# PSUM banks of different tiles used side by side in the experts and the last layers

## The chip, the cores and the metric

The kernel runs on one core of a Trainium2 chip. The metric is the time of one execution on the device, in microseconds (us); the lower the better. The engines are named as the profile names them: PE is TensorE (PEld its weight load), DVE is VectorE, ACT is ScalarE, POOL is GpSimd, and SP issues the transfers.

## What is computed

Attention with rotary embedding over 4 batches, 8 heads, 576 tokens and 64 elements per head; a soft mixture of 8 experts with 4 slots each over the 2304 tokens; and a two-layer MLP of 512 to 2048 to 512 with a squared ReLU. All in float32.

```python
def _moe_ref(x, phi, w1, w2):
    logits = x @ phi                                   # 2304 x 32
    d = softmax over tokens of logits                  # (written out with max, exp, sum)
    slot_input = (d.T @ x).reshape(8, 4, 512)
    for e in range(8):
        h = np.maximum(slot_input[e] @ w1[e], 0.0)     # 4 x 1024
        slot_out[e] = h @ w2[e]                        # 4 x 512
    c = softmax over slots of logits
    return c @ slot_out                                # 2304 x 512

def _moe2_ref(x, w_in, w_out):
    r = np.maximum(x @ w_in, 0.0)
    return (r * r) @ w_out
```

(The two softmax lines are shortened.)

## The kernel before

**Stages.** Sixteen pairs of heads go through attention until about 331 us. The experts follow until about 392 us, and the MLP runs to the end at 624.5. A planner orders the program: every step is handed to `op` with its engines and estimated times, a due time and what it reads and writes, and the planner emits one order for each engine. The key `("b", i)` stands for PSUM bank i in these lists, so a step is ordered after whatever used its bank before. Below the planner, the programming layer adds the semaphore waits between engines.

**PSUM.** There are eight banks of 512 float32 values in each of the 128 partitions. `PAIRS` are three tiles of two banks each; `BANKS[0]` and `[1]` are the halves of the first, `[2]` and `[3]` of the second, `[4]` and `[5]` of the third. `BANKS[6]` and `[7]` are tiles of one bank. The printed orders name the tiles `bank0_86`, `bank1_87`, `bank2_88` (the three pairs) and `obank0_89`, `obank1_90`; the profile writes `bank` and `obank` and leaves the numbers out.

**Experts, first layer.** r runs over four pairs of experts. Each has four groups `m1` of eight matmuls (L1089, k = 0 to 3) into bank r % 2, then a ReLU eviction by ACT (L1106), four transposes `tr` by PE (L1114) into bank 2 + r % 2 and two copies `keep` by DVE (L1125) into `si`.

**Combination weights.** Between these, `combine(b)` makes the softmax over the slots of batch b, in bank 5 or 6: transposes of the logits (L889, L890), a chain of small DVE operations from L895 to L908 with an exponential on ACT (L923), transposes back (L913) and an ACT copy (L919).

**Experts, second layer.** `second(r)` has for each r four groups `m2` of eight matmuls (L1149) into bank r % 2, which a memset (L1133) has zeroed, an ACT copy (L1164) and a product `ms` with the group sum (L1170) into bank 4. A DVE copy (L1185) ends the stage. Idle fill matmuls (L1435) into a spare bank stand at places that the planner chose.

**MLP.** `w_prime` multiplies slot outputs by w_in (L1231, then ACT L1246, PE L1247, ACT L1248, DVE L1243) in bank 5. `mlp1` makes 768 tokens of one block of 128 hidden columns in two halves (L1295) and evicts them (L1306) before L1314, L1323, L1325 and L1340 square and split them. `mlp2` adds into six banks, c = 0 to 5, 36 matmuls a step (L1364), and after every fourth step the six banks are evicted: by ACT in the first of four quarters (L1380), by DVE with an addition after (L1386). The output leaves from L1392.

**Transfers.** SP issues the weights in one queue, in the planner's order. The last ones are w2 of the last pair into tEb and tEa, 512 KB each in two parts, and behind them six loads of w_in and w_out, 1024 KB each.

Of the kernel before, what the change touches and what calls it, by code (L numbers as in the profile page):

```python
# [14 lines left out]
AF = mybir.ActivationFunctionType  # L15
# [161 lines left out]
def kernel(  # L177
# [85 lines left out]
    def f(ap):  # L263
        return ap.bitcast(F32)
# [613 lines left out]
    def combine(b, g, mem):  # L878
        (lc_of, lc_k), (rm_of, _), (rs_of, _), (ck_of, ck_k) = mem
        lg = lgs[b]  # L880
        bank, bk = BANKS[5 + b % 2], [("b", 5 + b % 2)]
        lc = lc_of().rearrange("p (a s) -> p a s", s=NSLOT)
        rm, rs = rm_of().unsqueeze(2), rs_of().unsqueeze(2)
        ck = ck_of().rearrange("p (c g s) -> p c g s", c=5, g=4)

        lt = bank.rearrange("p (c s) -> p c s", s=NSLOT)

        def o0(e):
            nc.tensor.transpose(bank[:, 0:128], lg[:, 0:128], ident)  # L889
            nc.tensor.transpose(bank[0:64, 128:160], lg[0:NSLOT, 128:192], ident[0:NSLOT, 0:NSLOT])  # L890

        def o1(e):
            for a, cs in ((128, slice(0, 4)), (64, slice(4, 5))):
                t = lt[0:a, cs]
                nc.vector.tensor_reduce(out=rm[0:a, cs], in_=t, op=ALU.max, axis=AX.X)  # L895
                nc.vector.tensor_tensor(
                    out=lc[0:a, cs], in0=t, in1=rm[0:a, cs].to_broadcast(list(t.shape)), op=ALU.subtract
                )

        def o2(e):  # L900
            nc.vector.tensor_reduce(out=rs, in_=lc, op=ALU.add, axis=AX.X)
# [14 lines left out]

        def o4(t0, m):
            t0 += S * b
            nc.scalar.activation(out=cst_of()[:, t0 : t0 + m], in_=bank[:, 0:m], func=AF.Copy)  # L919

        op({"PE": 0.2}, o0, g, [("lg", b, n) for n in (4, 1)] + ["ident"], bk)
        op({"DVE": 0.8}, o1, g, bk, [lc_k])
        op({"ACT": 0.25}, lambda e: nc.scalar.activation(out=lc, in_=lc, func=AF.Exp), g, (), [lc_k])  # L923
        op({"DVE": 1.6}, o2, g, (), [lc_k, ck_k])
        for cs, t0, m in ((range(4), 0, 512), ((4,), 512, 64)):
            op({"PE": 0.11 * len(cs)}, lambda e, cs=cs: o3(cs), g, [ck_k, "ident"], bk)
            op({"ACT": 0.05 + m / 1100}, lambda e, t0=t0, m=m: o4(t0, m), g, bk, [("cst", b, t0)])
# [60 lines left out]
    def experts():  # L988
# [90 lines left out]

        for r in range(4):  # L1080
            w, wk, wslots = w_of("w1", r)
            bk = r % 2

            for k in range(4):

# [26 lines left out]
            def tr(e, hs_of=hs_of, bk=bk):  # L1112
                for k in range(4):
                    nc.tensor.transpose(  # L1114
                        BANKS[2 + bk][:, 128 * k : 128 * k + 128], hs_of()[:, 128 * k : 128 * k + 128], ident
                    )

            op({"PE": 0.5}, tr, g + r + 0.5, [hs_k, "ident"], [("b", 2 + bk)])

            def keep(e, bk=bk, r=r):  # L1120
                t = BANKS[2 + bk].rearrange("p (k j s) -> p k j s", k=4, j=4)
# [7 lines left out]
            op({"DVE": 0.25}, keep, g + r, [("b", 2 + bk), ht_k], [(ht_k, r)])  # L1129
        free("A1", g + 3.5, after=last)  # L1130

        for bk in range(2):
            op({"DVE": 0.5}, lambda e, bk=bk: nc.vector.memset(BANKS[bk], 0.0), g + 5, (), [("b", bk)])  # L1133
        for b in range(B):
            combine(b, g + 0.3 + 0.4 * b, cks[b % 2])

        def second(r):


            bk = r % 2  # L1140
            hs_of, hs_k = hs[bk]
            for j in range(4):
                w_of, wk, wslot = where["w2", 2 * r + j // 2, j % 2]

                def m2(e, j=j, w_of=w_of):
                    if r == 2:
                        spare_bank[:] = [aux[:, 0:128]]
                    for q in range(4):
                        nc.tensor.matmul(  # L1149
                            BANKS[bk][32 * q : 32 * q + 8, :],  # L1150
                            lhsT=ht_of()[:, r, q, 8 * j : 8 * j + 8],
                            rhs=w_of()[:, q, :],
                            start=(j == 0),
                            stop=(j == 3),
                        )
# [12 lines left out]
            def ms(e):  # L1168
                for k in range(4):
                    nc.tensor.matmul(  # L1170
                        BANKS[4][:, 32 * k + 8 * r : 32 * k + 8 * r + 8],
                        lhsT=hs_of()[:, 128 * k : 128 * k + 128],
                        rhs=gsum[:, 0:8],
                        start=True,
                        stop=True,
                    )

            op({"PE": 0.75}, ms, g + 10 + r, [hs_k], [("b", 4)], wait=WAIT)

        for r in range(4):  # L1180
            second(r)
        g += 30
        start = op(
            {"DVE": 0.2},
            lambda e: nc.vector.tensor_copy(out=sot, in_=BANKS[4][:, 0:128].rearrange("p (k s) -> p k s", k=4)),  # L1185
            g - 20, [("b", 4)], [("sit", 0), ("sit", 1)], wait=WAIT,
        )
        mlp(g + 2, sot, start)

# [4 lines left out]
    def mlp(g, sot, start):  # L1194
# [24 lines left out]
        def w_prime(n, due, c0=0, c1=512):  # L1219
# [20 lines left out]
            wk = sorted({wst_k(n, c // 128) for c in range(c0, c1, 128)}, key=str)  # L1240

            def low(e):
                nc.vector.tensor_tensor(out=o()[64:], in0=BANKS[5][64:, c0:c1], in1=f(o())[64:], op=ALU.subtract)  # L1243

            op({"PE": 0.1 + 0.85 * z}, m1, due, [("sit", 0), ("sit", 1)] + [cs[n % 2][h][1] for h in halves], [("b", 5)], wait=wait)
            op({"ACT": 0.05 + 0.45 * z}, lambda e: nc.scalar.activation(out=ws_of()[:, c0:c1], in_=BANKS[5][:, c0:c1], func=AF.Copy), due, [("b", 5)], [ws_k], wait=wait)  # L1246
            op({"PE": 0.02 + 0.85 * z}, lambda e: nc.tensor.matmul(BANKS[5][:, c0:c1], lhsT=gsum, rhs=ws_of()[:, c0:c1], start=True, stop=True), due, [ws_k], [("b", 5)], wait=wait)  # L1247
            op({"ACT": 0.05 + 0.45 * z}, lambda e: nc.scalar.activation(out=o(), in_=BANKS[5][:, c0:c1], func=AF.Copy), due, [("b", 5)], wk, wait=wait)  # L1248
            op({"DVE": 0.07 + 0.535 * z}, low, due, [("b", 5)], wk, wait=wait)

        def wst_k(n, q):
            return wst_key if n == 0 and q == 0 else ("wst", n, q // 2)
# [28 lines left out]
        def mlp1(n):  # L1281
# [6 lines left out]
            due, wait = (g + n - AHEAD, 0.0) if n else (g - 20, WAIT)  # L1288
            reads = [wst_k(fc // 4, fc % 4)] + [("cst", b, x) for b in range(B) for x in (0, 512)]
            for h in range(2):  # L1290
                i = 4 if one and n else 3 if one and h else 4 + h
                t0 = TT * t + 384 * h
                op(
                    {"PE": 0.17},
# [48 lines left out]
                    due, sk, gk, wait=wait,  # L1343
                )

        PO = [0, 1, 2, 3, 6, 7]

        def mlp2(n):
            q, t, fc = steps[n]
# [6 lines left out]
            for c in range(6):  # L1356

                def mm(e, c=c):
# [3 lines left out]
                    for i, (x, y) in enumerate(((0, 0), (0, 1), (1, 0))):  # L1362
                        for z in (slice(0, 256), slice(256, 512)):
                            nc.tensor.matmul(  # L1364
                                BANKS[PO[c]][:, z],
                                lhsT=gt[:, x, 128 * c : 128 * c + 128],
                                rhs=wo[:, fc % 2, y, z],
                                start=(fc % FQ == 0 and i == 0 and z.start == 0),
# [1 line left out]
                                skip_group_check=z.start > 0,  # L1370
                            )

                op({"PE": 0.7}, mm, g + n, [(gt_k, c // 3)] + wo_reads, [("b", PO[c])])
                if fc % FQ < FQ - 1:
                    continue
                o_of, o_k = sums[6 * t + c]
                if q == 0:
                    op(
                        {"ACT": 0.5},
                        lambda e, o_of=o_of, c=c: nc.scalar.activation(out=o_of(), in_=BANKS[PO[c]], func=AF.Copy),  # L1380
                        g + n, [("b", PO[c])], [o_k],
                    )
# [141 lines left out]
```

## Time and profile before

| | before |
|---|---|
| median of 3 runs | 629.14 us (625.99 to 629.26) |
| profiled execution | 626.27 us |
| its span in the trace | 624.5 us |
| PE busy | 94% |
| DVE, ACT, POOL busy | 62%, 45%, 35% |
| experts stage | about 338 to 392 us |
| MLP | about 392 to 624.5 us |

The span counts from the first to the last instruction of the trace; 1.8 us of the execution lie around it. The rows further down come from several views. A timeline row has a start, a duration, the engine, the line, the operation and its tiles, and a count of merged instructions; in brackets stands how long the engine was idle before and whom it waited for. The wait view adds up such idle times by line. The chain of work follows the work that ended last back through whatever released it. A window row has busy times of each engine in a stretch, then PE's clock, the DMA share and the rate.

### The profile page before, as it was taken

The numbers are of one execution on the slowest core, as the hardware profiler recorded it, in microseconds if no ns is written. First come the engines' busy times: TensorE is split into PE (matmuls) and PEld (weight loads), VectorE is DVE, ScalarE is ACT, GpSimd is POOL, SyncE is SP. The second block draws the span as 40 slices with busy tenths as digits, with TensorE's granted clock in tenths as the row PEclk, the third lists the DMA queues.
The fourth block names the chain that finished last, engine by engine and source line by source line (L and its number), as shares of the span: only waits on it lengthen the run. The fifth ranks groups of instructions, "written<-read, shape, count | busy, mean of one in ns | idle before, by whom it ended". The sixth has DMA issues, their size and how long they took to land.

```text
span 624.5 us, 13406 instructions
## 1 busy us (share of the span) xinstructions
PE 585.9 (94%) x5535; PEld 429.5 (69%) x5535; DVE 384.9 (62%) x818; ACT 278.9 (45%) x492; POOL 215.6 (35%) x168
## 2 busy tenths in 40 slices
PE   1899999999999999999997989999999999999997
PEld 1556555566555665555654324789999999999996
DVE  3476666766657666666534714998487569355543
ACT  1235444444344443453431313788484456444440
POOL 1999998538866668660110000000000000000000
PEclk9799999999999999999999999999999999999999
DMA  9546854574356331322538999333210030000222
GB/s 188 132 95 179 216 133 140 142 209 104 116 137 165 78 90 47 83 89 75 212 137 297 365 390 394 117 131 135 69 68 1 1 119 17 1 1 2 102 103 101
DMA packets 36253, 80.90 MB, mean 130 GB/s; under 512 B 7616, under 2 KB 8032, under 8 KB 35168
## 3 DMA queue, kind: packets, MB, share of 16 engines
q1 hardware_dynamic: 34704, 77.98, 40.9%
q10 hardware_dynamic: 1488, 2.06, 1.7%
q8 instruction: 43, 0.70, 0.5%
q14 instruction: 18, 0.15, 0.1%
HBM read 75.24 MB, written 4.72 MB: 128 GB/s over the span
## 4 chain that ended last, share of the span: by engine, by line
PE 73%; DMA 8%; DVE 7%; POOL 6%; ACT 2%; issue 2%; SPq 1%; ACTq 0%; DVEq 0%; POOLq 0%
PE bank L1364 21%; PE obank L1364 10%; PE obank L477 10%; PE bank L443 8%; POOL arena L320 4%; PE bank L495 4%; DMA arena<-in_qk_dram 3%; PE bank L391 3%; PE bank L1295 3%; PE bank L1149 2%; PE bank L447 2%; DVE mcol L398 2%; DMA tEb<-mrow 2%; PE bank L1089 2%; POOL tLb L320 1%
## 5 line engine op out<-in xcount | busy, mean ns | idle before, releaser
L456 ACT ACTIVATE tO<-bank 128x576 f32<-128x576 f32 (+1 forms) x160 | 99.5, 647 | 157.1 <-PE bank L447 136.4
L398 DVE TENSOR_REDUCE mcol<-bank 128x2 f32<-128x576 f32 x160 | 115.5, 748 | 53.3 <-PE bank L391 53.0
L320 POOL TENSOR_TENSOR arena<-arena 128x576 f32<-128x576 f32 x90 | 125.3, 1413 | 53.9 <-DMA arena<-in_qk_dram 53.6
L477 PE MATMUL obank<-tO,pb 128*64 128x288 f32 x640 | 104.8, 426 | 2.8 <-DVE pb L519 1.6
L1364 PE MATMUL bank<-w,tEb 128*128 128x256 f32 x576 | 72.8, 279 | 1.2 <-ACT w__927 L1380 1.1
L1364 PEld LDWEIGHTS bank<-w,tEb 128*128 128x128 f32 x576 | 70.0, 188 | 3.5 <-ACT w__927 L1380 1.4
L464 POOL TENSOR_TENSOR pb<-tO 128x576 f32<-128x576 f32 x32 | 45.2, 1413 | 36.8 <-ACT tO L456 36.8
L477 PEld LDWEIGHTS obank<-tO,pb 128*64 128x64 f32 x640 | 34.9, 135 | 31.8 <-issue 17.1
L1306 ACT ACTIVATE pb<-bank 128x384 f32<-128x384 f32 x48 | 22.1, 493 | 47.4 <-PE bank L1295 35.5
L501 DVE STREAM_TRANSPOSE bank<-bank 128x288 f32<-128x288 f32 x32 | 15.9, 498 | 44.2 <-PE bank L495 44.2
L495 PE MATMUL bank<-tO,ones 128*32 128x288 f32 x384 | 37.5, 410 | 0.0
L1364 PE MATMUL obank<-w,tEb 128*128 128x256 f32 x288 | 37.1, 277 | 0.0
L1306 ACT ACTIVATE arena<-bank 128x384 f32<-128x384 f32 x48 | 21.6, 489 | 33.1 <-PE bank L1295 31.4
L1364 PE MATMUL bank<-w,tEa 128*128 128x256 f32 x288 | 36.4, 280 | 0.0
L443 PE MATMUL bank<-tEb 64*128 64x288 f32 x200 | 35.5, 352 | 0.4 <-ACT tO L456 0.3
L1364 PEld LDWEIGHTS bank<-w,tEa 128*128 128x128 f32 x288 | 34.9, 188 | 1.4 <-issue 1.2
L1364 PEld LDWEIGHTS obank<-w,tEb 128*128 128x128 f32 x288 | 35.1, 188 | 0.0
L1364 PE MATMUL bank<-w,tO 128*128 128x256 f32 x288 | 35.0, 276 | 0.0
L1364 PEld LDWEIGHTS bank<-w,tO 128*128 128x128 f32 x288 | 34.6, 188 | 0.0
L443 PEld LDWEIGHTS bank<-tEb 64*128 64x128 f32 x200 | 18.7, 184 | 20.7 <-issue 11.3
L391 PE MATMUL bank<-tEb 64*128 64x288 f32 x200 | 29.7, 334 | 0.7 <-DVE mcol L398 0.5
L443 PE MATMUL bank<-tLb,tEb 64*128 64x288 f32 x200 | 29.5, 292 | 0.0
(286 smaller groups left out, 1097.2 us busy)
## 6 DMA issues: line engine op xcount, KB each, us to landing
arena<-in_qk_dram SPq DMA_DIRECT2D x15, 576.0 KB
arena<-in_qk_dram SPq DMA_DIRECT2D x14, 512.0 KB
pb<-in_v_dram SPq DMA_DIRECT2D x16, 320.0 KB
arena<-in_w_dram SPq DMA_DIRECT2D x8, 512.0 KB
tLb<-in_w_in_dram SPq DMA_DIRECT2D x3, 1024.0 KB
pb<-in_w_in_dram SPq DMA_DIRECT2D x3, 1024.0 KB
w__415<-in_w_dram SPq DMA_DIRECT2D x4, 512.0 KB
w__591<-in_w_dram SPq DMA_DIRECT2D x4, 512.0 KB
```

What stands on the lines that cost most here:

```text
L320: ENG[e].tensor_tensor(out=o, in0=x, in1=y, op=how)
L391: nc.tensor.matmul(on_ring(tok)[:, j, 0:HQ], lhsT=hi[rows, 1, UNIT[u]], rhs=hi[rows, 0, HALF[h]], start=True, stop=True)
L398: lambda e: nc.vector.tensor_reduce(out=mcol[:, h, :, u], in_=on_ring(tok)[:, :, 0:HQ], op=ALU.max, axis=AX.X),
L443: nc.tensor.matmul(st[:, j, 0:HQ], lhsT=k[x][rows, UNIT[u]], rhs=q[y][rows, HALF[h]], start=(i == 0), stop=False)
L456: lambda e: nc.scalar.activation(out=pr[0:m], in_=on_ring(tok)[0:m, :, 0:HQ], func=AF.Exp, scale=0.125),
L464: lambda e: nc.gpsimd.tensor_tensor(out=acc, in0=one, in1=pr, op=ALU.add),
L477: nc.tensor.matmul(o_t[rows, 0:HQ], lhsT=vr[:, u, j, :], rhs=pr[:, j, :], start=(u == 0), stop=(u == 4))
L495: nc.tensor.matmul(sm[QUAD[2 * j + w], 0:HQ], lhsT=ones[:, 0:32], rhs=xs_[2 * i + w][:, j, :], start=(i == 0), stop=(i == 1))
L501: {"DVE": 0.47}, lambda e: nc.vector.transpose(out=on_ring(tok)[:, 1, 0:HQ], in_=on_ring(tok)[:, 0, 0:HQ]),
L1295: lambda e, i=i, t0=t0: nc.tensor.matmul(BANKS[i][:, 0:384], lhsT=wst_of()[:, 128 * fc : 128 * fc + 128], rhs=cst_of()[:, t0 : t0 + 384], ...
L1306: lambda e, i=i, h=h: nc.scalar.activation(out=rg_of()[:, 0, h], in_=BANKS[i][:, 0:384], func=AF.Relu),
L1364: nc.tensor.matmul(BANKS[PO[c]][:, z], lhsT=gt[:, x, 128 * c : 128 * c + 128], rhs=wo[:, fc % 2, y, z], start=(fc % FQ == 0 and i == 0 and ...
```

## The change

Only PSUM banks change, and the place of one memset. The first layer uses banks 0 and 2 in turn, and the transposes banks 1 and 3. `combine` takes the two one-bank tiles, 6 and 7, and its first step is also ordered after the second half of the slot inputs. The second layer takes banks 4 and 0 in turn; bank 4's memset is due ahead of combine, bank 0's stays with the later ones. `ms` and `w_prime` go to bank 7, `mlp1` to bank 6 in the first quarter (its very first step takes 5 as well) and to 6 and 7 after it, and `mlp2` to banks 0 to 5 in place of 0, 1, 2, 3, 6, 7.

```diff
@@ combine
-        bank, bk = BANKS[5 + b % 2], [("b", 5 + b % 2)]
+        bank, bk = BANKS[6 + b % 2], [("b", 6 + b % 2)]
...
-        op({"PE": 0.2}, o0, g, [("lg", b, n) for n in (4, 1)] + ["ident"], bk)
+        op({"PE": 0.2}, o0, g, [("lg", b, n) for n in (4, 1)] + ["ident", ("sit", 1)], bk)
@@ experts, first layer
-            bk = r % 2
+            bk = 2 * (r % 2)
...
-                        BANKS[2 + bk][:, 128 * k : 128 * k + 128], hs_of()[:, 128 * k : 128 * k + 128], ident
+                        BANKS[1 + bk][:, 128 * k : 128 * k + 128], hs_of()[:, 128 * k : 128 * k + 128], ident
...
-        for bk in range(2):
-            op({"DVE": 0.5}, lambda e, bk=bk: nc.vector.memset(BANKS[bk], 0.0), g + 5, (), [("b", bk)])
+        LATER = (4, 0)
+        for bk, due in zip(LATER, (g + 0.2, g + 2.2)):
+            op({"DVE": 0.5}, lambda e, bk=bk: nc.vector.memset(BANKS[bk], 0.0), due, (), [("b", bk)])
@@ second
-            bk = r % 2
-            hs_of, hs_k = hs[bk]
+            bk = LATER[r % 2]
+            hs_of, hs_k = hs[r % 2]
...
-                        spare_bank[:] = [aux[:, 0:128]]
+                        spare_bank[:] = [BANKS[2][:, 0:128]]
@@ ms, and the copy that ends the stage
-                        BANKS[4][:, 32 * k + 8 * r : 32 * k + 8 * r + 8],
+                        BANKS[7][:, 32 * k + 8 * r : 32 * k + 8 * r + 8],
@@ w_prime (all its uses of bank 5)
-                            BANKS[5][32 * k : 32 * k + 32, a:b],
+                            BANKS[7][32 * k : 32 * k + 32, a:b],
@@ mlp1
-                i = 4 if one and n else 3 if one and h else 4 + h
+                i = 6 if one and n else 5 if one and h else 6 + h
@@ mlp2 (PO[c] becomes c at all its uses)
-        PO = [0, 1, 2, 3, 6, 7]
-                                BANKS[PO[c]][:, z],
+                                BANKS[c][:, z],
```

The order of steps on each engine stays as it was but for one memset on DVE. What differs is the tiles and with them the waits. From line 1133 on, lines of the new kernel count one higher until the line `PO` is gone.

First place: PE at the first layer's r=1 (L1089 with w4 and w6 are k=0 and k=1, L1114 the transposes of r=0). Before:

```order
L1089 MATMUL bank0_86<-w4__1113,sit0_118 32x512 x2
L1089 MATMUL bank0_86<-w6__1473,sit0_118 32x512 x2
L1089 MATMUL bank0_86<-w4__1113,sit0_118 32x512 [waits Activation_49]
L1089 MATMUL bank0_86<-w4__1113,sit0_118 32x512
L1089 MATMUL bank0_86<-w6__1473,sit0_118 32x512 x2
L1114 MATMUL bank1_87<-ident_61,arena_76 128x128 [waits DMAHW7_49,DMAHW0_49]
L1114 MATMUL bank1_87<-ident_61,arena_76 128x128 x3
```

Now:

```order
L1089 MATMUL bank1_87<-w4__1113,sit0_118 32x512 x2
L1089 MATMUL bank1_87<-w6__1473,sit0_118 32x512 x2
L1089 MATMUL bank1_87<-w4__1113,sit0_118 32x512 x2
L1089 MATMUL bank1_87<-w6__1473,sit0_118 32x512 x2
L1114 MATMUL bank0_86<-ident_61,arena_76 128x128 [waits DMAHW7_49,DMAHW0_49,Activation_49]
L1114 MATMUL bank0_86<-ident_61,arena_76 128x128 x3
```

The wait for ACT has moved from the middle of r=1's first groups to the transposes behind them.

Second place: PE in the second layer, where the last group of r=0 is followed by the first of r=1 and by `ms` of r=0. Before:

```order
L1149 MATMUL bank0_86<-pb_84,si_66 8x512 [waits DMAHW1_49]
L1149 MATMUL bank0_86<-pb_84,si_66 8x512
L1149 MATMUL bank0_86<-pb_84,si_66 8x512 [waits DMAHW6_49,Activation_49]
L1149 MATMUL bank0_86<-pb_84,si_66 8x512
L1149 MATMUL bank0_86<-pb_84,si_66 8x512 [waits DMAHW7_49]
L1149 MATMUL bank0_86<-pb_84,si_66 8x512
L1170 MATMUL bank2_88<-gsum_62,arena_76 128x8 x4
```

Now (L1150 and L1171 are L1149 and L1170 of before):

```order
L1150 MATMUL bank2_88<-pb_84,si_66 8x512 [waits DMAHW1_49]
L1150 MATMUL bank2_88<-pb_84,si_66 8x512
L1150 MATMUL bank0_86<-pb_84,si_66 8x512 [waits DMAHW6_49,DVE_49]
L1150 MATMUL bank0_86<-pb_84,si_66 8x512
L1150 MATMUL bank0_86<-pb_84,si_66 8x512 [waits DMAHW7_49]
L1150 MATMUL bank0_86<-pb_84,si_66 8x512
L1171 MATMUL obank1_90<-gsum_62,arena_76 128x8 [waits Activation_49]
L1171 MATMUL obank1_90<-gsum_62,arena_76 128x8 x3
```

The wait for ACT stands at `ms` and no longer at r=1's first group, which now waits for DVE (the memset of bank 0).

Third place: DVE behind combine's last chain (L908 of b=3), with the copies L1125 of r=2 and r=3. Before:

```order
L908 TENSOR_TENSOR tEb2_120<-tEb2_120 128x5x32 [waits DVE_49]
L908 TENSOR_TENSOR tEb2_120<-tEb2_120 128x5x32
L1133 MEMSET bank0_86 128x512 [waits Activation_49]
L1125 COPY si_66<-bank1_87 128x4x2x4 [waits PE_49]
L1125 COPY si_66<-bank1_87 128x4x2x4
L1133 MEMSET bank0_86 128x512 [waits Activation_49]
L1125 COPY si_66<-bank1_87 128x4x2x4 [waits PE_49]
L1125 COPY si_66<-bank1_87 128x4x2x4
```

Now:

```order
L908 TENSOR_TENSOR tEb2_120<-tEb2_120 128x5x32 [waits DVE_49]
L908 TENSOR_TENSOR tEb2_120<-tEb2_120 128x5x32
L1134 MEMSET bank0_86 128x512 [waits PE_49,Activation_49]
L1125 COPY si_66<-bank0_86 128x4x2x4 [waits DVE_49]
L1125 COPY si_66<-bank0_86 128x4x2x4
L1125 COPY si_66<-bank1_87 128x4x2x4 [waits PE_49,Activation_49]
```

One of the two memsets stood between the copies and is gone from here: it is bank 4's, and it now stands right behind L1072, ahead of the first L895. The other, of bank 0, waits for PE and ACT.

## Rows read from the trace of the kernel before

**Rows 1.** The page's first part: busy time and share of each engine.

```profile
PE 585.9 (94%) x5535; PEld 429.5 (69%) x5535; DVE 384.9 (62%) x818; ACT 278.9 (45%) x492; POOL 215.6 (35%) x168
```

**Rows 2.** Waits of PE, 338 to 392 us: total us, times, longest.

```profile
PE bank L1149 <- ACT arena L1164: 2.3, 3, 0.8
PE bank L1114 <- ACT arena L1106: 1.1, 2, 0.8
PE bank L1089 <- DVE bank L1133: 0.9, 1, 0.9
PE bank L1089 <- ACT arena L1106: 0.8, 1, 0.8
```

**Rows 3.** Timeline, PE, first layer at r=1: start, duration, operation, count.

```profile
344.92 0.60 PE L1089 MATMUL bank<-w__1113,sit 128*32 128x512 f32 x2
...
346.36 0.62 PE L1089 MATMUL bank<-w__1113,sit 128*32 128x512 f32 x2 [0.83 <-ACT arena L1106]
```

**Rows 4.** The chain of work, 353 to 366 us: start, duration, what.

```profile
353.20 0.30 DVE tLa L895
...
358.81 0.47 DVE tEb L908 x2
...
361.19 0.59 PE obank L913 x4
361.78 1.85 PE bank L1089 x16
```

**Rows 5.** Timeline, DVE, combine's first two batches.

```profile
343.24 0.29 DVE L895 TENSOR_REDUCE tLa<-bank 128x4 f32<-128x128 f32 x1 [2.69 <-PE bank L890]
...
348.12 0.29 DVE L1125 COPY si<-bank 128x32 f32<-128x32 f32 x2 [0.56 <-PE bank L1114]
```

**Rows 6.** Timeline, PE and ACT, second layer around r=0 to r=1, and its end.

```profile
367.15 1.04 PE L1149 MATMUL bank<-tLb,si 128*8 128x512 f32 x8
...
368.01 1.04 PE L1149 MATMUL bank<-pb,si 128*8 128x512 f32 x8
...
369.12 0.60 ACT L1164 ACTIVATE arena<-bank 128x512 f32<-128x512 f32 x1 [3.43 <-PE bank L1149]
...
369.76 1.04 PE L1149 MATMUL bank<-pb,si 128*8 128x512 f32 x8 [0.72 <-ACT arena L1164]
...
370.74 1.06 PE L1170 MATMUL bank<-gsum,arena 128*128 128x8 f32 x8
...
387.08 1.04 PE L1149 MATMUL bank<-tEa,si 128*8 128x512 f32 x8
```

**Rows 7.** Windows at the end of the stream of weights.

```profile
381.00:392.00 11.00, 10.86 (x88) 6.39 (x80) 5.20 (x7) 4.01 (x6) 0.00 (x0) 1.00 1.04 397
392.00:397.00 5.00, 4.17 (x36) 3.42 (x35) 4.88 (x10) 4.04 (x8) 0.00 (x0) 1.00 0.56 218
```

**Rows 8.** Window of the MLP's first 20 us.

```profile
392.00:412.00 20.00, 19.02 (x156) 16.67 (x156) 19.41 (x29) 15.41 (x27) 0.00 (x0) 1.00 0.40 132
```

**Rows 9.** Waits of PE, 392 to 456 us, without the longest.

```profile
PE bank L1295 <- DVE tO L1243: 0.4, 1, 0.4
PE bank L1231 <- ACT pb L1306: 0.4, 1, 0.4
```

**Rows 10.** Timeline, ACT and PE, the first evictions of the MLP.

```profile
417.50 1.55 ACT L1380 ACTIVATE w__927<-bank 128x512 f32<-128x512 f32 x3
...
418.13 3.00 PE L1364 MATMUL bank<-w,tEb 128*128 128x256 f32 x24 [1.13 <-ACT w__927 L1380]
```

**Rows 11.** Timeline, DVE and PE, evictions of c=4 and 5 in the steady part.

```profile
567.68 1.28 DVE L1386 TENSOR_TENSOR w__1643<-w__1643,obank 128x512 f32<-128x512 f32 x2
...
570.40 0.84 PE L1364 MATMUL obank<-w,tEb 128*128 128x256 f32 x6
```

**Rows 12.** Timeline, PE and DVE, the end.

```profile
618.46 1.52 PE L1364 MATMUL obank<-w,tO 128*128 128x256 f32 x12
619.87 1.28 DVE L1386 TENSOR_TENSOR w__1643<-w__1643,obank 128x512 f32<-128x512 f32 x2
```

More of the change, by code (lines that the diff above doesn't have):

```diff
@@ L1114, in tr @@
                     nc.tensor.transpose(
-                        BANKS[2 + bk][:, 128 * k : 128 * k + 128], hs_of()[:, 128 * k : 128 * k + 128], ident
+                        BANKS[1 + bk][:, 128 * k : 128 * k + 128], hs_of()[:, 128 * k : 128 * k + 128], ident
                     )
-            op({"PE": 0.5}, tr, g + r + 0.5, [hs_k, "ident"], [("b", 2 + bk)])
+            op({"PE": 0.5}, tr, g + r + 0.5, [hs_k, "ident"], [("b", 1 + bk)])
             def keep(e, bk=bk, r=r):
-                t = BANKS[2 + bk].rearrange("p (k j s) -> p k j s", k=4, j=4)
+                t = BANKS[1 + bk].rearrange("p (k j s) -> p k j s", k=4, j=4)
                 o = ht_of()[:, r].rearrange("p k (j s) -> p k j s", j=4)
@@ L1127, in keep @@
                     )
-            op({"DVE": 0.25}, keep, g + r, [("b", 2 + bk), ht_k], [(ht_k, r)])
+            op({"DVE": 0.25}, keep, g + r, [("b", 1 + bk), ht_k], [(ht_k, r)])
         free("A1", g + 3.5, after=last)
-        for bk in range(2):
-            op({"DVE": 0.5}, lambda e, bk=bk: nc.vector.memset(BANKS[bk], 0.0), g + 5, (), [("b", bk)])
+        LATER = (4, 0)
+        for bk, due in zip(LATER, (g + 0.2, g + 2.2)):
+            op({"DVE": 0.5}, lambda e, bk=bk: nc.vector.memset(BANKS[bk], 0.0), due, (), [("b", bk)])
         for b in range(B):
@@ L1176, in ms @@
                     )
-            op({"PE": 0.75}, ms, g + 10 + r, [hs_k], [("b", 4)], wait=WAIT)
+            op({"PE": 0.75}, ms, g + 10 + r, [hs_k], [("b", 7)], wait=WAIT)
         for r in range(4):
@@ L1184, in experts @@
             {"DVE": 0.2},
-            lambda e: nc.vector.tensor_copy(out=sot, in_=BANKS[4][:, 0:128].rearrange("p (k s) -> p k s", k=4)),
-            g - 20, [("b", 4)], [("sit", 0), ("sit", 1)], wait=WAIT,
+            lambda e: nc.vector.tensor_copy(out=sot, in_=BANKS[7][:, 0:128].rearrange("p (k s) -> p k s", k=4)),
+            g - 20, [("b", 7)], [("sit", 0), ("sit", 1)], wait=WAIT,
         )
@@ L1242, in low @@
             def low(e):
[L1243 to L1249, printed above, removed]
+                nc.vector.tensor_tensor(out=o()[64:], in0=BANKS[7][64:, c0:c1], in1=f(o())[64:], op=ALU.subtract)
+            op({"PE": 0.1 + 0.85 * z}, m1, due, [("sit", 0), ("sit", 1)] + [cs[n % 2][h][1] for h in halves], [("b", 7)], wait=wait)
+            op({"ACT": 0.05 + 0.45 * z}, lambda e: nc.scalar.activation(out=ws_of()[:, c0:c1], in_=BANKS[7][:, c0:c1], func=AF.Copy), due, [("b", 7)], [ws_k], wait=wait)
+            op({"PE": 0.02 + 0.85 * z}, lambda e: nc.tensor.matmul(BANKS[7][:, c0:c1], lhsT=gsum, rhs=ws_of()[:, c0:c1], start=True, stop=True), due, [ws_k], [("b", 7)], wait=wait)
+            op({"ACT": 0.05 + 0.45 * z}, lambda e: nc.scalar.activation(out=o(), in_=BANKS[7][:, c0:c1], func=AF.Copy), due, [("b", 7)], wk, wait=wait)
+            op({"DVE": 0.07 + 0.535 * z}, low, due, [("b", 7)], wk, wait=wait)
         def wst_k(n, q):
@@ L1371, in mm @@
                             )
-                op({"PE": 0.7}, mm, g + n, [(gt_k, c // 3)] + wo_reads, [("b", PO[c])])
+                op({"PE": 0.7}, mm, g + n, [(gt_k, c // 3)] + wo_reads, [("b", c)])
                 if fc % FQ < FQ - 1:
@@ L1379, in mlp2 @@
                         {"ACT": 0.5},
-                        lambda e, o_of=o_of, c=c: nc.scalar.activation(out=o_of(), in_=BANKS[PO[c]], func=AF.Copy),
-                        g + n, [("b", PO[c])], [o_k],
+                        lambda e, o_of=o_of, c=c: nc.scalar.activation(out=o_of(), in_=BANKS[c], func=AF.Copy),
+                        g + n, [("b", c)], [o_k],
                     )
@@ L1385, in mlp2 @@
                         {"DVE": 0.68},
-                        lambda e, o_of=o_of, c=c: nc.vector.tensor_tensor(out=o_of(), in0=o_of(), in1=BANKS[PO[c]], op=ALU.add),
-                        g + n - 1, [("b", PO[c])], [o_k],
+                        lambda e, o_of=o_of, c=c: nc.vector.tensor_tensor(out=o_of(), in0=o_of(), in1=BANKS[c], op=ALU.add),
+                        g + n - 1, [("b", c)], [o_k],
                     )
```

## The prediction

> **What bounds the kernel now.** I read the page's first part first: TensorE is busy 585.9 of 624.5 us, 94% [rows 1]. A change that leaves the work of TensorE alone can win at most its idle time, so the question is where TensorE waits, and the wait view by stage answers it. In the experts stage (338 to 392 us) it names seven stops: three of the second layer on the eviction L1164 (2.3 us), two of the transposes L1114 on the eviction L1106 (1.1), one of the first layer on a memset (0.9) and one on L1106 (0.8), 5.1 us together and not one on a DMA [rows 2]. In the first quarter of the MLP (392 to 456) it names two of 0.4 us [rows 9], and one of 1.13 on an eviction [rows 10]. From 456 us on the same view is empty. So the gain, if there is one, lies in the experts stage, and what counts is how much of each stop is real once its neighbours are gone.
>
> What the stops have in common is seen by laying the bank numbers beside them: the waiting instruction and the one waited for touch different banks of one two-bank tile. The case at 346.36 shows it. The first layer of r=1 (bank 1) has issued k=0 and stands before k=1; ACT evicts r=0 from bank 0, and only then, 0.83 us idle, does TensorE go on [rows 3]. The order of before prints a wait on ACT just there. The eviction itself could have run earlier, but it too waited for the other bank's matmuls. In the order of after this wait is gone, and one on ACT stands at L1114, which really reads what ACT writes. Likewise the memset L1133 clears bank 0 while r=3, k=1 wants bank 1.
>
> **First layer.** A stop costs more than its idle time, because a series that restarts has to fill the pipeline again. Four matmuls of L1089 are followed by the next four after about 0.46 us (1.85 us for 16 in the chain) [rows 4]; at 344.92 four start, and the next start at 346.36, 1.44 us later [rows 3]: 0.98 lost for 0.83 of idle, so 0.15 on top for each stop. The four stops of this layer are then 1.1 + 0.9 + 0.8 = 2.8 us idle and 4 x 0.15 = 0.6 on top: 3.4 us. I take each as gone: r=1 and r=3 now use bank 2, the memset of bank 4 stands ahead of combine, that of bank 0 no longer shares a tile with what r=3 writes, and the transposes' eviction no longer waits for the next r.
>
> Not all of that arrives. The transposes of the combination weights (L913) wait for VectorE. Its chain for b=0 and b=1 began before the first stop and had one hole behind it, 0.56 us at L1125 [rows 5]; so it can move up by about 0.6 and no more, and the 0.98 of the first stop shrinks to about 0.7. For b=2 and b=3 the chain of work lies on VectorE itself, from L895 at 353.20 to the end of L908 at 358.81 + 0.47 = 359.28 [rows 4]. It begins behind L889 and moves up with it by these 0.7, to 358.6. TensorE comes to the L913 of b=3 at 361.19 now [rows 4]; freed of the two stops on the way (0.3 and 0.9 idle and 0.15 each on top, 1.5 us) and 0.7 earlier, it would come at about 359.0. That leaves 0.4 us, and it doesn't wait. **First layer: 3.1 us.** The early memset costs 0.48 us of VectorE, in the 2.69 us for which VectorE waits ahead of its first L895 [rows 5]: nothing.
>
> **Second layer.** Each r uses one bank for its four groups of eight matmuls, 0.86 us from one group to the next (367.15 to 368.01); from r=0 to r=1 it is 368.01 to 369.76, 1.75 [rows 6]: 0.89 lost for 0.72 idle. Three such stops, 2.3 us of idle [rows 2] and about 0.17 each on top: 2.8 us. After, r and r+1 lie in tiles 2 and 0, and the first group of r+1 need not wait for L1164. What comes next is L1170, the product with gsum, which truly needs L1164. It stands behind that first group: the group takes 0.98 (369.76 to 370.74), so L1170 would start 0.86 + 0.98 = 1.84 after the last group's start, and L1164 ends 1.11 + 0.60 = 1.71 after it (368.01 to 369.12, and 0.60) [rows 6]. The margin is 0.1 us, so this costs 0 to 0.1 each; I take 0. **Second layer: 2.8 us**, so 5.9 by the copy L1185 at the end of the stage.
>
> **The stream of weights is the next limit.** From 381 to 392 the DMA engines move 397 GB/s at a share of 1.04 [rows 7], that is, they are full, and TensorE's earlier reads can't make them faster. The last weights of the second layer are in tEa, used at 387.08 [rows 6]; 5.9 earlier is 381.2. Behind tEa come six loads of 1.05 MB, 6.29 MB. Bytes moved from 381 on: 11 x 397 = 4.37 MB, and 5 x 218 = 1.09 MB until they stop before 397 [rows 7], 5.46 MB. The other 0.83 MB takes 2.1 us, so tEa is complete at about 378.9. That leaves 2.3 us, less the time from the last byte to the signal, which no row here shows. The transfers stay hidden, but the gain of this stage can't go beyond 8.2 us.
>
> **First quarter of the MLP.** The stops of L1231 on L1306 and of L1295 on L1243, 0.4 each [rows 9], are between banks 4 and 5 of one tile, and the change puts these users into three places. Yet VectorE is busy 19.41 us of the 20 from 392 to 412 [rows 8], so TensorE soon waits for what it makes anyway. Ends: 0 if VectorE paces all of it, 1.0 if both stops and their restarts are won; I take 0.4, nearer to VectorE's row. The stop of 1.13 us at 418.13 stays: c=0 wants bank 0, ACT is still evicting c=1 from bank 1 (L1380, three from 417.50) [rows 10], and these two keep their tile.
>
> That last row bears on a rule. The trace shows TensorE waiting until the first of three evictions from 417.50 is done, though bank 0 was emptied earlier. The Trainium skill, PSUM — Partial Sum Buffer, section "PSUM bank collisions raise a hardware error", says that engines have to be kept apart by bank and quadrant, and that other pairs may run at once. By it c=0 needn't wait here, nor c=4 for c=5 after the change, and the tail term below would be 0. The trace disagrees: the waits go by tile, which is the program's doing, and no run here shows what the chip would stand.
>
> **MLP from 456 us, and the tail.** c=4 and c=5 move from tiles of their own into the two banks of tile 2. In the steady part this is covered: at the closest such place their evictions start at 567.68 and end 1.28 later at 568.96, and the next c=4 starts at 570.40 [rows 11], 1.4 us later. At the end the last matmuls of c=4 and c=5 run from 618.46 for 1.52, to 619.98, and the eviction of c=4 starts at 619.87 [rows 12]. It now has to wait for c=5: **minus 0.1 us.**
>
> **Sum:** 3.1 + 2.8 + 0.4 - 0.1 = 6.2 us, 1.0%. The profiled execution took 626.27 us in all, so 620.1. It lies at the low end of the runs (625.99, 629.14, 629.26); the same 6.2 from the median is 622.9. Without knowing which level most runs of after take, I use the mean of the four executions, 627.7, and predict 621.5.
>
> **Rivals.** (1) *VectorE and ACT take the gain back.* For it speaks the six microseconds for which the chain lies on VectorE [rows 4] and its full stretch from 392 [rows 8]; against it, the 0.4 us that I find left at L913. If the first layer gives only what the chain's hole gives, 0.6, and the MLP nothing, the gain is 0.6 + 2.8 - 0.1 = 3.3: about 624.4. Chance 0.14. (2) *The stream becomes the wait.* If the signal comes 3.2 us behind the last byte, tEa is usable at 382.1, the gain of the stage is 5.0 instead of 5.9, and the time about 622.4. For it speaks that the DMAs are full [rows 7], against it that TensorE had no wait on a DMA in this stage [rows 2]. Chance 0.06. (3) *Slower: the new pair c=4, c=5.* A price is shown by the pair that exists: 1.13 us idle at 418.13 [rows 10], about 1.3 with the restart. Twelve groups of evictions (four quarters of three token tiles) at that price are 15.6 us, against 6.2: 637 us. It decides once an eviction of c=5 ends later than the next step's c=4 starts; VectorE would have to come 1.4 us later than now at the closest place [rows 11]. Chance 0.03. (4) *The stops remain*, since the waits aren't where I read them or the next wait ends at the same time: no change, 627.7. The printed order, without these waits, speaks against it. Chance 0.05.
>
> **How the numbers follow.** The forecast, a gain of 5 to 7.5 us, has 0.72. What a measurement of this kernel can tell from no change is about 0.5%, 3.1 us. Faster by more: the forecast, (2), and two thirds of (1), 0.87. Within it: (4) and a third of (1), 0.10. Slower: 0.03. The range runs from the fastest level with a gain of 7.5 (625.99 - 7.5 = 618.5) to the slow level with rival (1) (629.2 - 3.3 = 625.9).
>
> **What would show it.** In the profile of after, the wait view of the experts stage has no L1149 on L1164 and no L1089 on an eviction or a memset; the starts from the last group of one r to the first of the next are 0.9 us apart; L1185 starts 5.9 us earlier; the eviction stop near 412 us is still there with about 1.1 us; from 450 us on nothing waits. A wait of L913 on VectorE over 0.5 us would speak for rival (1), a wait of L1149 on a DMA for rival (2), waits of L1364 on L1386 for rival (3). If L1185 comes 5.9 earlier but the end does not, I am wrong on what follows in the MLP.

## The result, and the profile after

The changed kernel takes 620.25 us (median of 4 runs, 619.85 to 621.97) against 627.6 us (4 runs, 625.99 to 629.26): the ratio on record is 0.9875, with a 95% interval of 0.9853 to 0.9897 (the two medians by themselves are 7.35 us apart, 0.9883). On another chip, later, the ratio was 0.990 (0.9871 to 0.9929). The forecast was 621.5 us, 6.2 us less than before.

Of the two profiled executions the spans are 624.5 and 618.1 us, 6.4 apart. The first part of the page of after answers to [rows 1]: PE has the same number of matmuls, and its share is a point higher.

```profile
PE 584.5 (95%) x5535; PEld 429.8 (70%) x5535; DVE 385.1 (62%) x818; ACT 279.7 (45%) x492; POOL 215.6 (35%) x168
```

The waits of PE in after, from 338 to 386 us, answer to [rows 2]. None of the seven stops is left; one new one of 0.3 has come, where the prediction let VectorE's chain take 0.3 back. The wait on L1020 lies ahead of the first layer.

```profile
PE obank L913 <- DVE tEb L908: 0.3, 1, 0.3
PE bank L1023 <- DVE xt L1020: 0.2, 1, 0.2
```

From 386 to 450 us the two lines that answer to [rows 9] and [rows 10] are these; L1296 is L1295 of before. The wait of L1231 on L1306 is gone, the other two stand. From 450 us on the view is empty in both kernels.

```profile
PE bank L1364 <- ACT w__927 L1380: 1.1, 1, 1.1
PE obank L1296 <- DVE tO L1244: 0.4, 1, 0.4
```

The place of [rows 3], first layer at r=1, reads in the timeline of after (start, duration, engine, line, operation, count):

```profile
345.21 0.60 PE L1089 MATMUL bank<-w__1113,sit 128*32 128x512 f32 x2
...
345.64 0.60 PE L1089 MATMUL bank<-w__1113,sit 128*32 128x512 f32 x2
```

Four matmuls now follow four after 0.43 us, where it was 1.44. The second layer, [rows 6], from r=0 to r=1 (L1150, L1165 and L1171 are L1149, L1164 and L1170 of before):

```profile
364.26 1.04 PE L1150 MATMUL bank<-tLb,si 128*8 128x512 f32 x8
365.12 1.90 PE L1150 MATMUL bank<-pb,si 128*8 128x512 f32 x16
366.29 0.60 ACT L1165 ACTIVATE arena<-bank 128x512 f32<-128x512 f32 x1 [3.65 <-PE bank L1150]
366.95 0.97 PEld L1171 LDWEIGHTS obank<-gsum,arena 128*128 128x128 f32 x8 [0.86 <-ACT arena L1165]
366.95 1.06 PE L1171 MATMUL obank<-gsum,arena 128*128 128x8 f32 x8
```

The last group of r=0 and the first of r=1 have grown into one series of 16. L1165 ends at 366.89, and L1171, whose weight load waited for it, starts at 366.95. PE shows no idle time ahead of it. The prediction had left 0.1 us between these two; it was 0.06, and it was enough.

To compare stages I take, in each trace, the start of the first L1089, the start of the copy that ends the experts (L1185; L1186 in after) and the start of the last eviction L1386. That gives the length of the experts and of most of the MLP, whatever attention took. The ends of the experts, before first, then after:

```profile
339.95 0.62 PE L1089 MATMUL bank<-w__415,sit 128*32 128x512 f32 x2
...
389.94 0.29 DVE L1185 COPY sit<-bank 128x128 f32<-128x128 f32 x1 [3.77 <-PE bank L1170]
```

```profile
340.24 0.62 PE L1089 MATMUL bank<-w__415,sit 128*32 128x512 f32 x2
...
384.23 0.29 DVE L1186 COPY sit<-obank 128x128 f32<-128x128 f32 x1 [2.84 <-PE obank L1171]
```

| kernel | experts, us | MLP to the last eviction, us |
|---|---|---|
| before | 339.95 to 389.94: 49.99 | to 619.87: 229.93 |
| after | 340.24 to 384.23: 43.99 | to 613.54: 229.31 |
| e9, after again | 342.94 to 386.92: 43.98 | to 616.25: 229.33 |

The experts give 6.0 us (forecast 5.9) and the MLP 0.6 (forecast 0.4 less 0.1 for the tail). Attention, which the change leaves alone, took 0.3 us more in the profiled execution of after.

### The profile page after: what moved, and what is told of

Its sections match the earlier page's. It is cut to its first block, busy times and chain, and to the rows that moved or that the text cites. A ratio compares the mean times of both kernels' runs of the same rounds, so it can differ in the third digit from the quotient of the medians.

```text
span 618.1 us, 13409 instructions
## 1 busy us (share of the span) xinstructions
PE 584.5 (95%) x5535; PEld 429.8 (70%) x5535; DVE 385.1 (62%) x818; ACT 279.7 (45%) x492; POOL 215.6 (35%) x168
## 4 chain that ended last, share of the span: by engine, by line
PE 55%; POOL 18%; DMA 14%; DVE 5%; issue 3%; SPq 3%; ACT 1%; ACTq 0%; DVEq 0%; POOLq 0%
PE bank L1364 31%; POOL arena L320 12%; DMA arena<-in_qk_dram 11%; PE obank L477 4%; PE bank L443 4%; POOL tLb L320 3%; PE obank L1296 3%; PE bank L1150 2%; SPq L312 2%; PE bank L1089 2%; PE bank L495 2%; POOL tLa L320 2%; DVE mcol L398 1%; DMA arena<-in_rope_dram 1%; POOL pb L464 1%
## 5 line engine op out<-in xcount | busy, mean ns | idle before, releaser
L1364 PE MATMUL bank<-w,tEb 128*128 128x256 f32 x864 | 106.1, 278 | 1.2 <-ACT w__927 L1380 1.1
L1364 PEld LDWEIGHTS bank<-w,tEb 128*128 128x128 f32 x864 | 103.3, 188 | 3.5 <-issue 1.6
L1364 PE MATMUL bank<-w,tEa 128*128 128x256 f32 x432 | 53.3, 279 | 0.0
L1364 PEld LDWEIGHTS bank<-w,tEa 128*128 128x128 f32 x432 | 51.7, 188 | 1.4 <-issue 1.2
L1364 PE MATMUL bank<-w,tO 128*128 128x256 f32 x432 | 51.3, 276 | 0.0
L1364 PEld LDWEIGHTS bank<-w,tO 128*128 128x128 f32 x432 | 50.9, 188 | 0.0
L1307 ACT ACTIVATE pb<-obank 128x384 f32<-128x384 f32 x47 | 21.7, 493 | 44.8 <-PE obank L1296 44.8
L1307 ACT ACTIVATE arena<-obank 128x384 f32<-128x384 f32 x48 | 21.6, 490 | 31.2 <-PE obank L1296 31.2
L443 PE MATMUL bank<-tEb,tLb 64*128 64x288 f32 x200 | 29.5, 291 | 0.0
L320 POOL TENSOR_TENSOR tLb<-arena,tEb 128x576 fp32r<-128x576 f32 x20 | 28.0, 1416 | 0.8 <-ACT tEb L350 0.7
```

The lines of the kernel that those rows point to most:

```text
L320: ENG[e].tensor_tensor(out=o, in0=x, in1=y, op=how)
L443: nc.tensor.matmul(st[:, j, 0:HQ], lhsT=k[x][rows, UNIT[u]], rhs=q[y][rows, HALF[h]], start=(i == 0), stop=False)
L1307: lambda e, i=i, h=h: nc.scalar.activation(out=rg_of()[:, 0, h], in_=BANKS[i][:, 0:384], func=AF.Relu),
L1364: nc.tensor.matmul(BANKS[c][:, z], lhsT=gt[:, x, 128 * c : 128 * c + 128], rhs=wo[:, fc % 2, y, z], start=(fc % FQ == 0 and i == 0 and z.s ...
```

## The experiments

**e1: the second layer in one tile.** The edit to the kernel after:

```diff
-        LATER = (4, 0)
+        LATER = (0, 1)
```

> The kernel after, but the second layer takes banks 0 and 1 of one tile in turn instead of 4 and 0; its order on PE, ACT and SP is that of after, only one memset stands later on DVE. My sum: the three stops of the second layer come back, about 0.75 us idle and 0.15 to 0.2 restart each, 2.8 us in all, so the copy that ends the experts stage comes 2.8 us (2.5 to 3.3) later than in after and the time is about 623. Rival (the stage is paced by the stream of weights or by VectorE): the stops come back but are swallowed behind them, under 1 us.

The ratio to before is 0.9943 (0.9918 to 0.9967). The experts take 342.50 to 389.36, 46.86 us: 2.87 more than after. The wait view of the stage has the three stops again, and PE idles in them for as long as in before:

```profile
PE bank L1150 <- ACT arena L1165: 2.3, 3, 0.8
PE obank L913 <- DVE tEb L908: 0.3, 1, 0.3
```

So each stop costs 0.96 us for 0.77 of idle time, 0.19 on top, and nothing swallowed it; that PE's restart takes the 0.19 is the prediction's reading, which no run takes apart. In its profiled execution attention ended 2.3 us later than in after, which is why the stage decides here and not the span.

**e2: the first layer in one tile.**

```diff
-            bk = 2 * (r % 2)
+            bk = r % 2
...
-                        BANKS[1 + bk][:, 128 * k : 128 * k + 128], hs_of()[:, 128 * k : 128 * k + 128], ident
+                        BANKS[2 + bk][:, 128 * k : 128 * k + 128], hs_of()[:, 128 * k : 128 * k + 128], ident
```

> The kernel after, but the first layer takes banks 0 and 1 and its transposes 2 and 3 as in the kernel before; the order is that of after on every engine. My sum: three of the four stops of the first layer come back, r=1 k=1 on L1106 (0.7 net, as VectorE's chain allows), the transposes of r=2 (0.35 to 0.45) and r=3 k=1 on the memset (0.95), 2.0 to 2.2 us; the stop of the transposes of r=3 stays away, since the second layer's r=0 lies in another tile. About 622.3. Rival (VectorE's chain gives and takes instead of the banks): 0.6 us or less.

Ratio 0.9939 (0.9918 to 0.996). The experts take 340.45 to 386.66, 46.21 us: 2.22 more than after. The waits are the three that were named, and the wait of L913 on VectorE is gone, since PE comes later to it:

```profile
PE bank L1089 <- DVE bank L1134: 0.9, 1, 0.9
PE bank L1089 <- ACT arena L1106: 0.8, 1, 0.8
...
PE bank L1114 <- ACT arena L1106: 0.3, 1, 0.3
```

**e8: both layers in one tile each**, the two edits together, since 2.87 and 2.22 leave 0.9 of the 6.0 open.

> Both layers of the experts in banks of one tile each (0 and 1, transposes 2 and 3, second layer 0 and 1), the rest as in the kernel after. The two alone lengthened the experts stage by 2.87 and 2.22 us, 5.1 together, of the 6.0 that the change saved. If the missing 0.9 is the stop of the transposes of r=3 on L1106, which either change removes, it appears here alone: the stage is 6.0 (5.8 to 6.2) longer than in after, about 50.0 us, and the wait view shows two stops of L1114. Rival (the 0.9 came from combine's banks or the early memset): 5.1.

The experts take 341.93 to 391.93, 50.00 us, 6.0 more than after, and the ratio to before is 0.9987 (0.9964 to 1.0011). The wait view is that of before line by line, with the second stop of L1114 back:

```profile
PE bank L1150 <- ACT arena L1165: 2.3, 3, 0.8
PE bank L1114 <- ACT arena L1106: 1.1, 2, 0.8
PE bank L1089 <- DVE bank L1134: 0.9, 1, 0.9
PE bank L1089 <- ACT arena L1106: 0.8, 1, 0.8
```

The second stop of L1114 is that of r=3. Its eviction was held by the second layer's first group, which wrote the other bank of its tile:

```profile
366.86 0.69 ACT L1106 ACTIVATE arena<-bank,den 128x512 f32<-128x512 f32 x1 [2.47 <-PE bank L1150]
```

It needs both layers in one tile for that, so either move frees it, and the two parts of the change don't add up from either side. The new banks of `combine` are still in place in e8, so by themselves they win nothing; what the two moves would give without them was not run.

**e3: memsets late.** A dependence on the first layer's r=2 holds both memsets:

```diff
+                if r == 2:
+                    held = last
...
-            op({"DVE": 0.5}, lambda e, bk=bk: nc.vector.memset(BANKS[bk], 0.0), due, (), [("b", bk)])
+            op({"DVE": 0.5}, lambda e, bk=bk: nc.vector.memset(BANKS[bk], 0.0), due, (), [("b", bk)], after=held)
```

> The kernel after, but both memsets are held until the first layer's r=2 has been computed, so that bank 4's stands behind combine on VectorE again. My sum: nothing on the way depends on it, 0 to 0.2 us against after, since its bank shares no tile with what r=3 writes. Rival (the early memset is what frees r=3): the 0.9 us stop of L1089 on the memset comes back, about 621.2.

Ratio 0.9896 (0.9863 to 0.9929), experts 340.80 to 384.79, 43.99 us, as after. VectorE's timeline has both memsets (L1136 there) at the end of the first layer:

```profile
359.48 0.48 DVE L1136 MEMSET bank<- 128x512 f32 x1
359.87 0.22 DVE L1127 COPY si<-bank 128x32 f32<-128x32 f32 x2
360.27 0.48 DVE L1136 MEMSET bank<- 128x512 f32 x1 [0.18 <-DVE si L1127]
```

So the early place of the memset is worth nothing by itself. What frees r=3 is that the bank to be cleared shares no tile with the bank that r=3 writes.

**e4: the MLP's banks of before** in the kernel after:

```diff
-                i = 6 if one and n else 5 if one and h else 6 + h
+                i = 4 if one and n else 3 if one and h else 4 + h
...
+        PO = [0, 1, 2, 3, 6, 7]
...
-                                BANKS[c][:, z],
+                                BANKS[PO[c]][:, z],
```

(and bank 5 in place of 7 in `w_prime`)

> The kernel after, but the MLP keeps the banks of the kernel before (its first product, the product with w_in and the six sums). My sum: the experts stage stays at after's length, the first quarter gives back 0.4 to 0.6 us, the tail wins 0.1, so 0.3 to 0.5 us above after. Rival (VectorE paces the first quarter anyway): 0, and with the tail 0.1 below after.

Ratio 0.9918 (0.9889 to 0.9947). Experts 340.32 to 384.30, 43.98; the MLP from there to the last eviction at 614.30, 230.00, which is 0.69 more than after, about that of before, and more than the 0.3 to 0.5 expected; the account of the first quarter of the MLP, further down, comes back to this. The stop of L1232 (L1231 of before) is back, with 0.4 of idle:

```profile
PE bank L1296 <- DVE tO L1244: 0.4, 1, 0.4
PE bank L1232 <- ACT pb L1307: 0.4, 1, 0.4
```

The tail shows in VectorE's last evictions: from the first of the last six to the fifth, e4 takes 2.56 us, after 2.72. The shared tile costs 0.16 at the end. First before, then e4, then after:

```profile
617.30 2.64 DVE L1386 TENSOR_TENSOR w__1473<-w__1473,bank 128x512 f32<-128x512 f32 x4 [6.18 <-PE bank L1364]
```

```profile
611.74 2.65 DVE L1388 TENSOR_TENSOR w__1473<-w__1473,bank 128x512 f32<-128x512 f32 x4 [6.19 <-PE bank L1366]
614.30 1.28 DVE L1388 TENSOR_TENSOR w__1643<-w__1643,obank 128x512 f32<-128x512 f32 x2
```

```profile
610.82 2.65 DVE L1386 TENSOR_TENSOR w__1473<-w__1473,bank 128x512 f32<-128x512 f32 x4 [6.36 <-PE bank L1364]
613.54 1.28 DVE L1386 TENSOR_TENSOR w__1643<-w__1643,bank 128x512 f32<-128x512 f32 x2
```

**e5 and e5b: the stop that is left.** L1364 still waits 1.13 us for c=1's eviction. In e5 the eviction of c=1 gets a due time one step earlier, in e5b all six:

```diff
-                        g + n, [("b", c)], [o_k],
+                        g + n - (c == 1), [("b", c)], [o_k],
```

> The kernel after, but in the first quarter of the MLP the eviction of c=1 gets an earlier due time, so that on ACT it stands right behind that of c=0; some other steps of ACT, VectorE and PE change places with it. If the stop of 1.13 us at the first evictions is c=0 waiting for the other bank of its tile, it goes: up to 1.3 us less from the copy that ends the experts to the end, about 619. Rival (the group needs ACT's or VectorE's other results at the same time): the wait moves to the input of L1364 and 0 to 0.3 is won.

> The same for all six evictions of the first quarter, whose due time is one step earlier, as it is in the later quarters; hardly any other step changes its place. If c=0 waits for c=1's bank alone, the stop of 1.13 us is gone or smaller by what the evictions move up, 0.8 to 1.3 us won. Rival: ACT's later steps (L1307, L1324) come late instead and L1364 waits for its input, so nothing is won.

Ratios 0.988 (0.9832 to 0.9927) and 0.9901 (0.9863 to 0.994); from after they can't be told apart. The stages tell more. From the copy to the last eviction e5 takes 389.14 to 618.14, 229.00 us, e5b 388.94 to 617.86, 228.92: 0.3 and 0.4 less than after, where 0.8 to 1.3 was expected of e5b. The stop of L1364 is gone in both, and in e5b half of it has come up at L1296, the first product of a later step (waits of PE, 390 to 450 us):

```profile
PE obank L1296 <- ACT arena L1307: 0.5, 1, 0.5
PE obank L1296 <- DVE tO L1244: 0.4, 1, 0.4
```

ACT does the evictions earlier, and L1307 later. In e5 the same wait shows 0.2 us. So both readings held in part: it was the other bank's eviction that was waited for, and then PE waits for ACT's later steps; what takes back the rest of the gain was not traced.

**e6: without the idle fill ahead of the last weights.** The fills ahead of the last groups of the second layer are left out, 18 matmuls that compute nothing needed:

```diff
-                    if r == 2:
+                    if r == 3 and j == 3:
                         spare_bank[:] = [BANKS[2][:, 0:128]]
```

> The kernel after without the idle fill matmuls of the second layer ahead of its last two pairs of groups (18 of them, 2.4 us of PE by their starts). If the weights are there as early as the bytes say (tEa complete at about 379 on this trace's clock), the copy that ends the experts comes up to 2.4 us earlier and no wait on a DMA shows. If the signal comes some 2 us behind the last byte, L1150 waits for a DMA ahead of tEa, and only 0.3 to 1.0 us is won; the wait's end then tells when the weights are usable, and so how much more the stage could have given. Rival: the granted clock falls without the fills and the time rises.

Ratio 0.9893 (0.9855 to 0.993). The experts take 344.70 to 388.38, 43.68: 0.31 less than after, for 2.4 us of fill. PE now waits for the weights, the two halves of tEa, and PE's clock stays at 1.00 of full speed in each window:

```profile
384.19 1.03 PE L1150 MATMUL bank<-tEa,si 128*8 128x512 f32 x4 [0.42 <-DMA tEa<-in_w_dram]
385.55 1.03 PE L1150 MATMUL bank<-tEa,si 128*8 128x512 f32 x4 [0.34 <-DMA tEa<-in_w_dram]
```

By the bytes moved, these weights should have been there earlier. The windows behind tEa show it (the last number is GB/s, the one ahead of it the DMA share):

```profile
385.00:390.00 5.00, 4.49 (x33) 2.64 (x32) 2.49 (x5) 1.94 (x3) 0.00 (x0) 1.00 1.04 399
390.00:395.00 5.00, 4.54 (x40) 3.71 (x38) 4.91 (x9) 3.88 (x9) 0.00 (x0) 1.00 1.04 398
395.00:400.00 5.00, 5.00 (x41) 4.20 (x41) 4.91 (x8) 3.94 (x7) 0.00 (x0) 1.00 0.92 353
400.00:405.00 5.00, 4.93 (x43) 4.60 (x43) 5.00 (x7) 3.69 (x6) 0.00 (x0) 1.00 0.32 63
```

Six loads of 1.05 MB stand behind tEa, 6.29 MB. From 385 to 400, 5.75 MB move, to 405, 6.07. So 0.2 to 0.5 MB of them moved ahead of 385, 0.6 to 1.4 us at 0.38 MB per us: by this count tEa is complete between 383.6 and 384.4, and PE could start at 385.55, 1.1 to 2.0 us later.

That is not the time from the last byte to its signal. The count takes the 16 DMA engines as one stream that fills tEa first and goes on only then, and they don't end together. Where the whole stream ends, the DMA share falls from 1.02 to nothing over some 1.8 us:

```profile
398.00:399.00 1.00, 1.00 (x11) 1.00 (x10) 1.00 (x2) 1.00 (x3) 0.00 (x0) 1.00 1.02 406
399.00:400.00 1.00, 1.00 (x9) 0.90 (x8) 0.94 (x3) 0.77 (x1) 0.00 (x0) 1.00 0.44 164
400.00:400.80 0.80, 0.73 (x6) 0.53 (x6) 0.80 (x2) 0.79 (x2) 0.00 (x0) 1.00 0.11 46
400.80:401.20 0.40, 0.40 (x5) 0.40 (x5) 0.40 (x1) 0.40 (x1) 0.00 (x0) 1.00 0.00 0
```

The trace also holds the signals, sixteen for each load, which I read as one from each engine. Those of tEa's second half come between 383.53 and 385.51, and PE starts 0.04 us behind the last of them. At the end of the stream the last packet ends at 400.81 and the last signal comes at 401.24. In the thirteen traces this distance is 0.41 to 0.59 us. So a signal is about 0.4 us behind its bytes, and most of the 1.1 to 2.0 us is the lag of the slowest engines, which a count of all bytes doesn't see.

**e7 and e10: both together**, e5b's evictions and no fill ahead of the last weights; e10 is e7 again, beside the kernel after (e9) on one chip.

> All six evictions one step earlier, and no fill ahead of the last weights. If both are independent, the sum of what the two give alone: 1 to 2 us below after, 618 to 619. Rival: the time won in the experts is lost at the start of the MLP, whose weights then are late.

> The kernel after once more, on the chip of the next run, for a direct comparison: 0.9875 of the kernel before, as measured first (0.985 to 0.990).

> The evictions of the first quarter one step earlier and no fill ahead of the last weights, beside the kernel after on the same chip. By the stages of its trace it is 0.85 us shorter than after, 0.14%, so 0.9860 if after gives 0.9875; less than the runs can tell apart.

e7: 0.9893 (0.9851 to 0.9936), experts 342.58 to 386.18, 43.60, MLP to the last eviction at 615.03, 228.85. e10: 0.988 (0.9845 to 0.9915), experts 343.58 to 387.51, 43.93, MLP to 616.41, 228.90. e9: 0.990 (0.9871 to 0.9929). The 0.4 us in the MLP come back in each execution; in the experts it is 0.4 us in e7 and 0.05 in e10. The expectations were higher: 1 to 2 us below after for e7, where the two stages give 0.85, and 0.85 for e10, where they give 0.48 against e9. Both are too small for the runs, and no version was found that beats after measurably.

## Why the prediction was right, point by point

**Where the time was.** The stops of PE in the experts were taken for waits between different banks of one tile, and e8 shows it: with the first order of banks back, and everything else of the change in place, the stage has its old length to 0.01 us and the old four lines of waits.

**First layer, forecast 3.1.** e1 keeps the first layer's part alone: 49.99 - 46.86 = 3.13 us. Its inner step held too: VectorE's chain took 0.3 back, at the L913 of b=1 (at 350.17 us), which waits 0.33 us in after. For b=3 the prediction left 0.4 us between VectorE and PE at L913, and no wait shows there.

**Second layer, forecast 2.8.** e1 against after gives 2.87, e2 against before 3.78. The sum put 0.9 for the transposes of r=3 on the first layer's account; e2 shows that the second layer's move would have freed it just as well. In the total it counts once, so 5.9 stood against 6.0, but the two terms are not independent as the sum had them.

**First quarter of the MLP, forecast 0.4.** Of the two stops that the prediction took for waits between banks 4 and 5, L1231 on L1306 was one and went. L1295 on L1243 stayed: L1243 writes `tO`, which L1295 reads, so the prediction had read a true dependence as one of banks. From the copy to the L1364 behind the stop of 1.13 us it takes 389.94 to 418.13 in before, 28.19 us, 384.30 to 412.46 in e4, 28.16, and 384.23 to 411.84 in after, 27.61: 0.55 to 0.58 won. The lead goes on growing in small steps, until some 52 us behind the copy, and then stays: the first of the last six evictions starts 227.36 us behind the copy in before, 227.44 in e4 and 226.59 in after. That is 0.77 won against before, which with the tail's 0.15 taken off gives the 0.6 of the table. The last 0.2 comes with the MLP's banks, since e4 lacks it, but the wait view names no stop for it, and its cause stays open. So the term lay within its ends of 0 and 1.0, and at 0.4 it was taken at half its size. VectorE, busy 19.80 of the first 20 us of the MLP in after (19.41 in before, [rows 8]), paces the stretch less strictly than that share suggested.

**The tail, minus 0.1.** It is 0.16 by e4 against after, 0.15 by before against after.

**The stream of weights: the step that was off.** The prediction had tEa complete at 378.9 us by the bytes, which left 2.3 us of margin, less the time to the signal, which it left open; rival (2) put its deciding point at 3.2 us behind that count. In before the last signal of tEa comes at 380.74, 1.8 us behind the count, and e6 shows why: the engines don't end together. In after the last signal comes at 380.34 and PE uses tEa at 381.37, so 1.0 us of margin was left, not 2.3; in e9, the same kernel, they are 383.95 and 384.06, 0.1 us apart. In e5, whose program for the experts is that of after, no margin is left: the signal comes at 386.28, the weight load of the second half waits for it, the last group takes 1.48 us where 1.04 is usual, and the stage 389.14 - 344.70 = 44.44 us:

```profile
385.88 1.48 PE L1150 MATMUL bank<-tEa,si 128*8 128x512 f32 x8
386.32 0.10 PEld L1150 LDWEIGHTS bank<-tEa,si 128*8 128x8 f32 x4 [0.34 <-DMA tEa<-in_w_dram]
```

So the change has brought the stage to its next limit: with 0 to 0.4 us more won (e10 and e7), the stream sets its end. Rival (2) had its mechanism right and was wrong by 1.4 us of lag. The Trainium skill, DMA: Bandwidth & Descriptors, section "Anatomy of one DMA — SWDGE (gpsimd) path", gives about 2.0 us of fixed cost for a transfer, most of it the receipt of the last write, for another way of issuing. The 1.8 us of before look like it, but in e6 only 0.4 us lie between the last packet and the last signal, so for SP's loads the trace doesn't bear that share out: the larger part goes with the spread of the engines.

**The rivals.** (1) VectorE took 0.3 us, not the rest. (3) c=4 and c=5 in one tile: no wait of PE on L1386 anywhere from 450 us on. (4) is refuted by the wait views.

**The level.** It is 620.25 against a forecast of 621.5. The ratio, 0.9875, is 7.8 us of 627.6, with 6.5 to 9.2 by its interval, while traces and the later comparison (0.990, 6.3 us) give 6.3 to 6.4. The sum was made on stages and hits that of the experts, 5.9 against 6.0; the MLP's 0.3 was 0.6. Which part of the first ratio is chance of attention's length I can't separate.

## What to carry to other kernels

When a wait in a trace joins two instructions that touch different data, look for what they share in the program's eyes: here a tile of two banks, and one such wait costs its idle time and 0.15 to 0.2 us on top. Put banks that are written and read at the same time into different tiles, and keep neighbours for what is used together. Then ask when the last of the DMA engines signals a transfer, not when the count of all bytes has it complete, before you say how much further a stage can shrink.

## What the runs showed of the hardware that was not expected

Attention, whose program is the same in all these kernels, ended anywhere from 339.95 to 344.97 us (start of the first L1089, thirteen profiled executions). PE's granted clock (the third number from the end) has a part in it: in before, after and e3, all three under 341 us, it stays at its upper level from 28 us on until the experts begin, and in e5b, the longest, it falls three times in that stretch. Two windows of after and the same two of its repetition e9:

```profile
150.00:160.00 10.00, 8.76 (x100) 5.24 (x100) 6.20 (x16) 4.77 (x9) 5.40 (x5) 1.00 0.91 225
160.00:170.00 10.00, 9.74 (x98) 5.92 (x98) 6.37 (x18) 3.65 (x6) 10.00 (x8) 1.00 0.11 35
```

```profile
150.00:160.00 10.00, 8.84 (x102) 5.33 (x100) 6.23 (x15) 4.87 (x9) 5.37 (x5) 1.00 0.92 223
160.00:170.00 10.00, 8.94 (x64) 5.17 (x64) 3.50 (x7) 2.50 (x4) 10.00 (x8) 0.66 0.11 35
```

From 150 to 160 us PE was busy 8.76 and 8.84 of 10 us, nearly alike; then the kernel after stays at 1.00, the upper level of 2.4 GHz, while e9 falls to a mean of 0.66, part of the time at 1.2 GHz, and gets through 64 matmuls instead of 98. No run here shows why one falls and the other doesn't. In the experts the clock is 1.00 in both, and the stage repeats to 0.02 us between executions (43.99, 43.98, 43.99 and 43.98 in after, e9, e3 and e4), though by the end of it the stream of weights can add 0.4. For a change of one stage, the stage's own length in the trace is a far finer measure than the time of the kernel.
